# Relu-squared attention into a gated feed-forward block: the input loads issued in another order, with another order of the work behind them

## The chip, the cores and the metric

The kernel runs on one core of one Trainium2 chip. The metric is the time of one execution on the device, in microseconds (us). The profile is taken by the hardware profiler from one execution. The engines are named as in the profile: PE is TensorE (matmuls; PEld is its weight load), DVE is VectorE, ACT is ScalarE, POOL is GpSimd, and SP is SyncE. SPq and POOLq are the DMA issues of SP and POOL.

## The reference: what is computed

```python
# q, k, v: (8 batches, 12 heads, 448 tokens, 64)
scores = (1 / sqrt(64)) * matmul(q, k.transpose(0, 1, 3, 2))
attn = maximum(scores, 0.0) ** 2 / 448
x = matmul(attn, v)                     # heads joined: x is (3584 tokens, 768)
g = x @ w_gate                          # (768, 1536)
val = x @ w_val                         # (768, 1536)
out = (gelu(g) * val) @ w_out           # (1536, 768) -> (3584, 768)
```

The inputs and the output are float32; the kernel converts to bf16 as it loads.

## The kernel before, in words

**Tiles.** A batch has 12 heads, which are handled in three *thirds* of four heads; (b, m) is third m of batch b. Queries and keys of a third lie in one tile `qk16` (queries in the upper 64 partitions, keys in the lower), of which there are two buffers (`RING_H`). Values lie in `v16`, three buffers. Gate and value weights are cut into six pairs `wg0`/`wv0` to `wg5`/`wv5` of 256 columns each, the output weights into four tiles `wo0` to `wo3`. All matmuls use a quarter of the array (64 x 64), and four of them, in two rows and two columns, run side by side: `PE0` and `PE1` in the code are the two rows.

**Stages.** The head dimension has to be on the partitions for the scores, so queries and keys are transposed. For batches 0 and 1 TensorE does it (L641, copied by DVE at L645 into `qkT`). From batch 2 on (`EARLY = 2`) DVE regroups `qk16` into `qkr` (L477), and SP issues two DMA transposes per third from `qkr` into `qkT` (L482). Then come, for each third, seven units of scores (L693), a relu on ACT (L708, two banks, 128 x 896), the square on DVE (L717), the values (L763), and the scaled copy into `xT` (L779 or L790). Batches 0 and 1 do the gate and value matmuls plainly (`add_gate_value`, L995, with the gelu at L1002 and the product at L1007). From batch 2 on, half of those matmuls are done for two batches at once in seven products instead of eight, with sums of the weights (`ws`) and of the tokens (`ts`). The output product (`add_product`) takes 256 tokens at a time, also in seven products, with sums of the output weights (`wt`, L1047, which need `wo0` and `wo2`, or `wo1` and `wo3`).

**What sets the order.** The kernel holds a planner, `run_plan` (L96). Every step is an `Op` with an engine, a cost, dependencies and a lag (the time from its end until another engine can use its result). The planner simulates the engines, always takes the step that can start earliest, and emits instructions in the order in which it takes them. Each engine then runs its own instructions in that order. For batch 0 the order on TensorE is fixed by hand. Behind it, units of work are taken from a list, `LINE` (L12): `s` is the next score unit (or TensorE transposes) of its batch in turn, `o` a values unit, a digit a gate or value unit of that batch, `4A1` and the like a unit of the seven products for two batches, and `a1` to `n7` a unit of an output product. The planner takes the first unit among the next 60 that is ready, or, if none is, the one that will be ready first. Score units are always taken in their own order.

**Loads.** POOL issues all input loads, in program order, so a load that waits holds up all loads behind it. The planner counts a load's arrival from its bytes (L269):

```python
        if op in arrivals:
            dma = max(dma, op.end) + arrivals[op]
            op.lag = dma + 2.0 - op.end
```

The DMA transposes have a fixed lag of 5.0 (L494), and the score units that use them a margin of 1.5 for batch 2 and 3.0 later (L727). Some loads wait: a `qk16` tile for the readers of the tile two thirds before (TensorE's transposes, or DVE's regrouping), and later thirds also for relus, as a pace (L1385 to L1393): queries and keys from (2, 2) on for the first two relus of the third three places before, values from (2, 0) on for the fourth and sixth relu of the third two places before.

The order of the loads before, behind those of batch 0, is written out in L1242 to L1263: pair 0; (1, 0) all; pair 1; queries and keys of (1, 1); pair 2; values of (1, 1); queries and keys of (1, 2); pair 3; values of (1, 2); pairs 4 and 5; queries and keys of (2, 0) and (2, 1); values of (2, 0); the four output weights; queries and keys of (2, 2); values of (2, 1); and so on in turn.

Of the kernel before, what the change touches and what calls it, by code (L numbers as in the profile page):

```python
# [9 lines left out]


LINE = """  # L12
0 1 4A1 s 1 s 1 0 o 2 5 1 1 o d1 s 4C5 1 1 1 0 o 0 0 c5 s 2C1 s s o 3 s 0 s a1 s 0 1 2B4 o 5 2 g2
o s 3 0 2 b7 s 1 o 6B6 o s s s a5 a7 s 4B1 2 d4 s 0 0 0 0 o s 0 a2 4D1 2C7 s s s o 2E1 2A5 0 2C6 s
2A6 0 0 0 0 b5 0 s s 2 0 s 1 0 s s 1 a6 4E5 d7 2B1 2E2 1 0 o g6 1 f1 s 1 a4 c4 s s 4A2 1 b6 s s
2B6 s s 1 2D3 s o s s o d3 o c2 6B1 s s s 1 s s s 1 b2 s s b1 s s 1 s 3 1 s 2D6 1 c7 a3 s s 2E3 o
f5 o o 2E6 1 g7 1 2F1 b4 s 2B2 s 2A3 b3 2B3 c1 s o s 2F2 4 s s i5 3 c3 4F5 s s c6 s 2 2E7 2C3 2
2B5 2D1 s s 2F3 e6 2B7 s s s 2 3 2 s 2A1 2 6F4 g4 2A2 s 2A7 4E4 s 2A4 s o s s 4 e4 3 o d5 s s o
2D7 2D4 4A5 2C5 o 2D2 s o h2 2C2 2F6 s 2F7 2E5 s 5 f6 2D5 j2 2 4 4A4 4F6 s s 2C4 2F5 e2 s s 5 s
2F4 o 3 o 3 6B5 2E4 h4 2 s 4C1 m6 3 s 3 d6 s 6B2 s 4 3 s s n2 f3 f4 s o d2 o 3 4B4 4A7 6E1 s s e1  # L20
6B7 e7 o o 4B3 g1 s 7 4 6D6 s o f2 s e3 s 6E3 s 5 e5 s 4 6D3 7 m3 4D4 4E7 s m4 f7 s s 4 m5 4A6 s s
5 4 4B6 s 4B2 s s g5 i1 4C2 o o s s 4D2 4 4 s j5 s s j3 j1 s 6C6 g3 5 i7 6 s k5 6A2 o 4B7 s 4F2 5
4D5 4C6 4E2 4E1 s s 4B5 4A3 s s 4D3 s 4E6 6C7 4C3 s 6C3 o 4F3 6A1 4C7 s 4D6 s n1 l4 o s 6A7 s 4 k3
4C4 6 s o h1 4E3 i3 4D7 s h7 6A6 6E7 6 i4 s 4F1 j6 6 o 4 4F4 s n3 s 5 4F7 s i6 s s n5 s s 6D1 6 s
5 h6 s 5 o s 6A5 7 7 6D2 o s s 5 s h5 l7 6 s s 6C4 s n7 s 6E4 6A3 s o 6C1 6E6 i2 o 6E2 7 j7 7 s h3
l5 s s s 6B3 s l1 j4 s 7 6F2 6 s 6C2 k6 o k7 6 6F1 6D7 m7 6B4 7 6A4 6 6 m1 6F7 6 n6 6F6 k4 l2 6E5
m2 l6 k1 6 6D4 7 7 l3 7 7 6C5 6F3 6D5 6F5 n4 k2
"""


class Op:

    def __init__(self, engine, cost, emit, deps=(), lag=0.0, prio=0, other=None):
        self.engine, self.cost, self.emit, self.prio = engine, cost, emit, prio
        self.deps = [d for d in deps if d is not None]
        self.lag = lag
        self.other = other
        self.takes = None
        self.margin = 0.0
        self.after = None  # L40
        self.gates = []
        self.start = self.end = None
        self.place = 0
        self.open = False

# [50 lines left out]
def run_plan(queues, pools, units, banks, arrivals, together, fill):  # L96

    free = {e: 0.0 for e in (*queues, *pools)}
    at = {e: 0 for e in queues}
    dma = last = floor = busy = 0.0  # L100
# [108 lines left out]
    while left:  # L209
        best = None  # L210
        for e, ops in queues.items():
            if at[e] < len(ops):
                r = ready(ops[at[e]])
                if r is not None:
                    t = max(r, free[e], floor if e in together else 0.0)
                    key = (t, 0, free[e])
                    if best is None or key < best[0]:
                        best = (key, e, ops[at[e]])
        whole = at["PE0"] == len(queues["PE0"])
        if whole or at["PE0"] >= fixed:  # L220
            found = next_unit(not whole)
            if found is not None:
                key = (found[0], -1, free["PE0"])
                if best is None or key < best[0]:
                    best = (key, "PE0", found)
        for e, ops in able.items():
            mine = None
            for op in ops:
                r = ready(op)
                if r is not None:  # L230
                    t = max(r, free[e], floor if e in together else 0.0)
                    key = (t, op.prio, free[e], op.place)
                    if mine is None or key < mine[0]:
                        mine = (key, e, op)
            if mine and (best is None or mine[0][:3] < best[0][:3]):
                best = mine
        assert best is not None, "the plan is stuck"
        (t, *_), e, op = best
        if isinstance(op, tuple):
            _, u, k = op  # L240
            u.begun = True
            units.remove(u)
            for x in u.grabs:
                x.takes[0].ask(*x.takes[1:])
            if u.chain is not None:
                opened.add(u.chain)
                if u.name[-1] in "234":
                    opened.discard(u.chain)
            if k is not None:
                u.box["k"] = k  # L250
                banks[k] = u.closer()
            queues["PE0"][at["PE0"]:at["PE0"]] = u.los
            for n, hi in enumerate(u.his):
                hi.place, hi.open = u.los[0].place + n, True
                if not need[hi]:
                    able["PE1"].append(hi)
            op = u.los[0]
        if op.other is not None and e != op.engine:
            op.engine, op.cost, op.emit = op.other
        op.start = t  # L260
        op.end = t + op.cost
        free[e] = op.end
        if e in together:
            floor = t
            if t > busy:
                fill(busy, t)
            busy = max(busy, op.end)
        if op in arrivals:
            dma = max(dma, op.end) + arrivals[op]  # L269
            op.lag = dma + 2.0 - op.end  # L270
        if e in at:
            at[e] += 1
        else:
            for x in homes[op]:
                able[x].remove(op)
        if op.takes is not None:
            op.takes[0].take(*op.takes[1:])
        op.emit()
        for user in users.get(op, ()):
            need[user] -= 1  # L280
            if not need[user]:
                offer(user)
        last = max(last, op.end)
        left -= 1
# [4 lines left out]
def kernel(  # L289
# [21 lines left out]
    NM = NPAIR // 2  # L311
# [5 lines left out]
    FC = d_ff // 128  # L317
    WCH = 256
    NW = d_ff // WCH
# [3 lines left out]
    WOG = 3  # L323
# [2 lines left out]
    FB = 4  # L326
    FILL = 30.0
    EARLY = 2
    WO_AT = 2, 2, 2, 2

    NP = 3
    RING_V, RING_T, RING_H, RING_L, RING_A, RING_O, RING_E = 3, 3, 2, 2, 4, 4, 5
# [73 lines left out]
    def load_w12(i):  # L406
        cols = slice(i * WCH, (i + 1) * WCH)

        def emit(wt, src):
            return nc.gpsimd.dma_start(  # L410
                wt[:, :, :], src[:, cols].rearrange("(c p) f -> p c f", p=128))
        w12_op[i] = [load(4 * d_model * WCH, lambda wt=wt, src=src: emit(wt, src))
                     for wt, src in ((wg[i], moe_w_gate), (wv[i], moe_w_val))]
# [6 lines left out]
    def load_qk(b, i, h0, h1, deps=()):  # L420

        src = (q, k)[i]
        m, r0 = divmod(h0, 4)

        def tile_of():
            if (b, m) not in qk16:
                qk16[b, m] = hpool.tile([128, 4, SC * D], bf16, name="qk16", tag="qk16")
            return qk16[b, m][HALF[i], r0:r0 + h1 - h0, :]

        op = load(4 * (h1 - h0) * S * D, lambda: nc.gpsimd.dma_start(  # L430
            tile_of(), src[b, h0:h1].rearrange("h (p c) d -> p h (c d)", c=SC)),
            deps, rate=400e3 if b else 300e3)
        qk_loads.setdefault((b, m), []).append(op)
        for pr in range(h0 // 2, h1 // 2):
            head_op[b, pr, i] = op
# [14 lines left out]
            for pr in range(h0 // 2, h1 // 2):  # L450
                head_op[b, pr, 2 + i] = op

    def load_heads(b, h0, h1):
        load_qk(b, 0, h0, h1)
        load_qk(b, 1, h0, h1)
        load_v(b, h0, h1)

    qkT, tr_op = {}, {}

    def qkT_tile(b, m):  # L460
# [7 lines left out]
    def add_dma_transposes(b, m, deps=()):  # L468
# [12 lines left out]
        def emit_transpose(c0, c1):  # L481
# [3 lines left out]
            if b > EARLY and c0 or m and b == EARLY:  # L485
# [3 lines left out]
        n = len(regrouped)  # L489
# [2 lines left out]
        copy.margin = 3.0  # L492
        tr_op[b, m] = [Op("SP", 0.19 * 2 * (c1 - c0), lambda c0=c0, c1=c1: emit_transpose(c0, c1),
                          [copy], lag=5.0) for c0, c1 in ((0, VC), (VC, SC))]  # L494
        qk_used[b, m] = [copy]
        t_made[b, m] = [*tr_op[b, m]]
        if m or b > EARLY:
# [741 lines left out]
        if h0 > 2:  # L1239
            load_v(0, h0 - 4, h1 - 4)  # L1240
    load_v(0, 8, 12)
    load_w12(0)  # L1242
    load_heads(1, 0, 4)
    load_w12(1)
    load_qk(1, 0, 4, 8)
    load_qk(1, 1, 4, 8)
    load_w12(2)
    load_v(1, 4, 8)
    load_qk(1, 0, 8, 12)
    load_qk(1, 1, 8, 12)  # L1250
    load_w12(3)
    load_v(1, 8, 12)
    load_w12(4)
    load_w12(5)
    late = [(b, m) for b in range(2, B) for m in range(NM)]
    for n, (b, m) in enumerate(late):
        for i in range(FC // WOG):
            if WO_AT[i] == n:
                load_wo(i)
        for i in range(2):  # L1260
            load_qk(b, i, 4 * m, 4 * m + 4)
        for b_, m_ in late[n - 1:n] + (late[n:] if n == len(late) - 1 else []):
            load_v(b_, 4 * m_, 4 * m_ + 4)  # L1263
    add_weight_sums()
    for b, m in late:
        add_dma_transposes(b, m)
# [202 lines left out]
```

## Time and profile before

| | before |
|---|---|
| runs shown | 411.26, 412.3, 685.4 us; median 412.3 |
| the profiled execution | 411.88 us, of which the span of the profile is 410.1 |
| PE busy | 392.3 us (96%), 8477 instructions |
| DVE busy | 298.5 us (73%) |
| ACT busy | 244.8 us (60%) |
| POOL busy | 74.1 us (18%) |
| loads' queue (q0) | 24.39 MB in 37152 packets, 46.3% of 16 engines' span |
| stores' and transposes' queue (q1) | 19.08 MB in 37888 packets, 24.1% |
| chain that ended last | PE 91%, DMA 5% |
| mean granted TensorE clock | 0.985 |

The times are those of a whole execution; all places in time further on are counted from the start of the span. A row of the timeline gives the start, the duration, the engine, the line, the operation with what it writes and reads, the count, and in brackets how long the engine had been idle before and what released it. PE counts as busy while any matmul is in flight, so its share says nothing of how many of the four quarters are in use.

### The profile page before, as it was taken

To read this page: it belongs to the slowest core of one execution; us is meant where nothing else is said; L and a number is where in the kernel's file an instruction comes from. 1 tells how busy PE (TensorE), PEld (TensorE's weight loads), DVE (VectorE), ACT (ScalarE), POOL (GpSimd) and SP (SyncE) were. 2 spreads that over 40 slices of the span, in tenths; PEclk is the share of its full clock that TensorE was granted. 3 is DMA by queue.
4 is the path that set the end of the run, shared out by engine and by line. 5 is a ranking of instruction groups with operands and counts; after the bars stand their busy time and mean duration, and the time that the engine had idled before them with its cause. 6 is when DMAs were issued, how large, how long until landed. Compare 5 with 4: busy or idle time off the path is not lost.

```text
span 410.1 us, 18547 instructions
## 1 busy us (share of the span) xinstructions
PE 392.3 (96%) x8477; PEld 348.1 (85%) x8480; DVE 298.5 (73%) x513; ACT 244.8 (60%) x366; POOL 74.1 (18%) x120
## 2 busy tenths in 40 slices
PE   7999996499999999999999999999999999999994
PEld 3566785399989899989998999999999999989993
DVE  2976776198677978788877777688998766577562
ACT  5947783167677667786666676677776733242220
POOL 7756350111212211110111111111110000000000
PEclk9999999599999999999999999999999999999999
DMA  8999999987899799636498987765331411000245
GB/s 108 190 200 197 198 206 180 122 103 105 131 124 136 119 192 154 93 49 71 56 136 127 158 169 116 122 63 81 54 48 42 118 42 40 4 3 3 65 113 136
DMA packets 75278, 44.84 MB, mean 109 GB/s; under 512 B 36160, under 2 KB 71744, under 8 KB 75200
## 3 DMA queue, kind: packets, MB, share of 16 engines
q0 software_dynamic: 37152, 24.39, 46.3%
q1 hardware_dynamic: 37888, 19.08, 24.1%
q8 instruction: 66, 1.08, 1.1%
q10 hardware_dynamic: 160, 0.20, 0.1%
q14 instruction: 12, 0.10, 0.1%
HBM read 48.76 MB, written 11.01 MB: 146 GB/s over the span
## 4 chain that ended last, share of the span: by engine, by line
PE 91%; DMA 5%; ACT 1%; issue 1%; DVE 1%; SPq 0%; POOL 0%; POOLq 0%
PE ff L375 80%; PE sp L375 8%; DMA qkT<-qkr 4%; PE ff L562 1%; ACT attnT L708 1%; PE sp L641 1%; DMA qk<-in_k_dram 1%; PE ff L641 0%; DVE qkT L645 0%; DVE attnT L717 0%; PE ff L604 0%; ACT gel L1002 0%; DVE osb L1196 0%; SPq L482 0%; ACT qkT L612 0%
## 5 line engine op out<-in xcount | busy, mean ns | idle before, releaser
L375 PE MATMUL ff<-xT,wg 64*64 64x448 bf16 x1872 | 195.4, 351 | 0.0
L708 ACT ACTIVATE attnT<-sp 128x896 bf16<-128x896 f32 x168 | 151.6, 922 | 55.8 <-PE sp L375 53.4
L375 PE MATMUL ff<-xT,wv 64*64 64x448 bf16 x1440 | 156.3, 352 | 0.2 <-issue 0.2
L375 PEld LDWEIGHTS <-wv 64*64 64x64 bf16 x1872 | 115.3, 107 | 8.6 <-issue 0.9
L375 PEld LDWEIGHTS <-wg 64*64 64x64 bf16 x1872 | 113.7, 107 | 9.0 <-issue 0.2
L717 DVE TENSOR_TENSOR attnT<-attnT 128x1792 bf16<-128x1792 bf16 (+1 forms) x98 | 92.3, 953 | 12.6 <-ACT attnT L708 11.9
L375 PE MATMUL sp<-qkT 64*64 64x448 bf16 (+1 forms) x768 | 79.7, 330 | 10.1 <-DMA qkT<-qkr 9.0
L375 PEld LDWEIGHTS <-s 64*64 64x64 bf16 x1344 | 80.2, 107 | 4.4
L375 PE MATMUL ff<-attnT,v 64*64 64x448 bf16 (+1 forms) x768 | 83.7, 326 | 0.1
L375 PE MATMUL ff<-wo,s 64*64 64x384 bf16 x672 | 60.9, 323 | 0.0
L375 PE MATMUL ff<-wt,s 64*64 64x384 bf16 x672 | 60.8, 323 | 0.0
L1007 DVE TENSOR_TENSOR uT<-gel,ff 128x448 bf16<-128x448 bf16 x60 | 37.0, 617 | 31.2 <-PE ff L375 27.0
L375 PEld LDWEIGHTS <-uT 64*64 64x64 bf16 x912 | 55.2, 107 | 2.1
L375 PEld LDWEIGHTS <-qkT 64*64 64x64 bf16 x768 | 39.4, 106 | 16.5 <-issue 7.5
L445 POOL DMA_DIRECT2D v<-in_v_dram x48 | 29.5, 619 | 128.6 <-ACT attnT L708 98.2
L375 PE MATMUL ff<-ts,wv 64*64 64x448 bf16 x432 | 51.5, 349 | 0.0
L375 PE MATMUL ff<-ts,ws 64*64 64x448 bf16 x432 | 51.1, 349 | 0.0
L375 PEld LDWEIGHTS <-v 64*64 64x64 bf16 x768 | 46.9, 106 | 4.0 <-issue 1.0
L375 PE MATMUL ff<-wo,uT 64*64 64x384 bf16 x576 | 49.9, 323 | 0.0
L1002 ACT ACTIVATE gel<-ff 128x448 bf16<-128x448 f32 x60 | 32.5, 544 | 27.0 <-PE ff L375 26.9
L375 PEld LDWEIGHTS <-ws 64*64 64x64 bf16 x648 | 41.1, 106 | 2.3
L924 DVE TENSOR_TENSOR part<-ff,part 128x448 f32<-128x448 f32 x54 | 32.9, 620 | 11.8 <-PE ff L375 7.0
(60 smaller groups left out, 374.7 us busy)
## 6 DMA issues: line engine op xcount, KB each, us to landing
out_dram<-osb SPq DMA_DIRECT2D x54, 192.0 KB, 3.6
v<-in_v_dram POOLq DMA_DIRECT2D x48, 128.0 KB, 3.9
qk<-in_q_dram POOLq DMA_DIRECT2D x23, 224.0 KB, 4.9
qk<-in_k_dram POOLq DMA_DIRECT2D x23, 224.0 KB, 5.9
wg<-in_moe_w_gate_dram POOLq DMA_DIRECT2D x6, 384.0 KB, 10.3
wv<-in_moe_w_val_dram POOLq DMA_DIRECT2D x6, 384.0 KB, 11.2
wo<-in_moe_w_out_dram POOLq DMA_DIRECT2D x4, 576.0 KB, 13.5
qkT<-qkr SPq DMA_TRANSPOSE x36, 5.3
```

The source lines that it names most:

```text
L375: return nc.tensor.matmul(o, lhsT, rhs, start=start, stop=stop, skip_group_check=onto, tile_position=(P * row, P * col))
L445: return nc.gpsimd.dma_start(v16[b, m][HALF[i], :, :, :], v[b, h0:h1].rearrange("h (p c) d -> p h c d", c=SC)[:, :, c0:c0 + VC, :])
L562: nc.tensor.matmul(t[:, :], warm[:, 0:128], warm[:, :], start=True, stop=True)
L641: nc.tensor.transpose(t[HALF[j], c, :], src[:, 2 * r + j, c, :], ident[:, :], tile_position=(0, P * j))
L708: relu.ins = nc.scalar.activation(duo["a"][:, u % 2, :, :], box[0][:, :, 0:S], AF.Relu).ins
L717: nc.vector.tensor_tensor(a[:, part], a[:, part], a[:, part], op=ALU.mult)
L924: rd.ins = nc.vector.tensor_tensor(t[:, :], box[0][:, 0:S], t[:, :], op=ALU.add).ins
L1002: nc.scalar.activation(gel[b, fc][:, :], box[0][:, 0:S], AF.Gelu)
L1007: u_op[b, fc].ins = nc.vector.tensor_tensor(uT[b][:, fc, :], gel.pop((b, fc))[:, :], box[0][:, 0:S], op=ALU.mult).ins
```

## The change: what it does

1. The order of the loads behind batch 0 is read from a new string, `LOADS`. A `w` is the next pair of gate and value weights, `o` the next output weight in the order 0, 2, 1, 3, `q` the queries and keys of the next third from (1, 0) on, and `v` the values of the next third. Read out, it begins: pair 0; queries and keys of (1, 0) and (1, 1); values of (1, 0); pair 1; values of (1, 1); queries and keys of (1, 2) and (2, 0); pairs 2 and 3; values of (1, 2); queries and keys of (2, 1); pair 4; values of (2, 0); queries and keys of (2, 2); pair 5; values of (2, 1); output weight 0; queries and keys of (3, 0) and (3, 1); values of (2, 2); output weight 2; values of (3, 0); queries and keys of (3, 2); output weights 1 and 3; queries and keys of (4, 0) and (4, 1); and on. What each load waits for is as before.
2. The planner's lag of the DMA transposes is no longer fixed: if the loads counted so far keep the DMA queue busy beyond the end of the issue, the rest of that time is added (`queued`).
3. `LINE`, the order of the units, is replaced as a whole. It holds the same units.
4. `load_heads` and `WO_AT` go, as nothing uses them now. Each load gets a `token`, which nothing else uses.

```diff
 LINE = """
-0 1 4A1 s 1 s 1 0 o 2 5 1 1 o d1 s 4C5 1 1 1 0 o 0 0 c5 s 2C1 s s o 3 s 0 s a1 s 0 1 2B4 o 5 2 g2
...
+a6 4A4 4C4 s o 2 1 s g2 0 s 3 2C5 s 0 d3 o 0 2C1 4C1 s 1 4B6 s o s 0 0 0 s s 0 0 s s 0 s 2B2 s 2
...
+LOADS = """
+w q q v w v q q w w v q w v q w v o q q v o v q o o q q v q v q v v q v v q v q v q v q v q v q v
+q v v
 """
...
+        self.queued = False
...
         if op in arrivals:
             dma = max(dma, op.end) + arrivals[op]
             op.lag = dma + 2.0 - op.end
+        elif op.queued:
+            op.lag += max(0.0, dma - op.end)
...
+        for op in tr_op[b, m]:
+            op.queued = True
...
     late = [(b, m) for b in range(2, B) for m in range(NM)]
...
+    todo = {"w": [*range(NW)], "o": [0, 2, 1, 3], "q": [(1, m) for m in range(NM)] + late,
+            "v": [(1, m) for m in range(NM)] + late}
+    for x in LOADS.split():
+        n, at = len(POOL), todo[x].pop(0)
+        if x == "w":
+            load_w12(at)
+        elif x == "o":
+            load_wo(at)
+        elif x == "v":
+            load_v(at[0], 4 * at[1], 4 * at[1] + 4)
+        else:
+            for i in range(2):
+                load_qk(at[0], i, 4 * at[1], 4 * at[1] + 4)
+        for op in POOL[n:]:
+            op.token = x, at
+    assert not any(todo.values())
```

More of the change, by code (lines that the diff above doesn't have):

```diff
@@ L12 @@
 LINE = """
-0 1 4A1 s 1 s 1 0 o 2 5 1 1 o d1 s 4C5 1 1 1 0 o 0 0 c5 s 2C1 s s o 3 s 0 s a1 s 0 1 2B4 o 5 2 g2
[L14 to L27, printed above, removed]
+a6 4A4 4C4 s o 2 1 s g2 0 s 3 2C5 s 0 d3 o 0 2C1 4C1 s 1 4B6 s o s 0 0 0 s s 0 0 s s 0 s 2B2 s 2
+a2 b1 o 3 s 3 s 0 0 0 s 1 o s s 4B7 2B1 b4 0 0 0 1 0 0 s o s s s b5 a4 s b6 1 0 0 0 c2 f3 1 a7 o o
@@ new lines @@
+1 2B6 s s s 1 0 1 2C2 s s 2 2A3 s 1 1 2A5 2 1 f4 g4 s s s s 2E6 s 1 a3 c1 s 4 o 1 1 s f5 2B3 s 0 s
+d1 o s o 1 s 2F3 s s s s 1 2D1 1 1 c6 2D4 1 2F1 3 c3 2A1 s 6 c5 s 2F4 a1 2 s o 1 1 4C6 o o 2B4 a5
+1 2A2 1 s s b7 o 2D6 b3 s s e7 s d6 s s 2 s o c7 o b2 3 o 2 s 2A7 s 2B5 s 2B7 s o 2E4 s s s 2E2 s
+2 s 4A1 2D2 s s 4A2 2F5 s s 2C7 s 2A4 3 s c4 s e2 e4 o s 6B2 2F7 o 2 4F2 4B1 3 s 5 s 2D3 3 e1 s
+2F2 s 2E1 2A6 s 2F6 2E5 4B5 s 2C4 2D7 2C6 o 2D5 4B3 5 6 k4 s d5 d4 s l3 s f1 s o e5 4A5 2 d7 s 4
+4E4 2C3 2 g5 3 s h3 2E7 g6 s 6B4 o 2 s 4D1 o g7 s f2 3 s 2E3 f6 s 5 s 4 o d2 o e3 f7 4 s s s s 4
@@ new lines @@
+4D2 3 s e6 6A6 4 o s 6F1 4D7 s 4 4F6 3 6B1 g1 s s 4E1 s s l4 i1 6E6 o 4A3 4A6 4F5 4F4 o 6A4 o s g3
+s s h4 4D5 4C7 4A7 l7 i6 4E2 o n7 s o s 6C3 s 6B7 s s s 4 4B4 s s o 6 h2 6 6E5 s 4E5 s 5 4 4D3 4D4
+s s 7 o 7 6C7 s s s 4 s s s 4B2 4E7 s 6D5 5 4D6 6A3 h5 4E6 j6 m1 s 5 6 5 s s i3 4C5 5 l6 4 h7 s
+6F5 h1 4C2 6B3 l2 4F1 s 6F2 4C3 5 6B6 s n3 4 6D1 4F3 j1 4E3 k7 4F7 6C1 5 o s j3 6D6 o s m4 s 5 o
+6C5 o s i5 j5 i7 5 i4 6 s o i2 6E7 s j7 7 s 6B5 s 6 s m3 m5 6A7 s h6 s 6F7 6A1 j2 6D7 s s k3 s s o
+6 s s s m2 7 6A5 o n5 6F6 7 l5 j4 n4 6C2 s n6 s m7 m6 k1 k6 6A2 6 6F3 6 n2 7 6D2 6D4 k5 7 6E1 6C6
@@ L28 @@
+l1 6E2 6 7 6 6D3 7 6F4 7 7 k2 7 n1 6E3 6E4 6C4
+"""
+LOADS = """
+w q q v w v q q w w v q w v q w v o q q v o v q o o q q v q v q v v q v v q v q v q v q v q v q v
+q v v
 """
@@ L328 @@
     EARLY = 2
-    WO_AT = 2, 2, 2, 2
     NP = 3
@@ L451, in load_v @@
                 head_op[b, pr, 2 + i] = op
[L453 to L456, printed above, removed]
     qkT, tr_op = {}, {}
@@ L1241 @@
     load_v(0, 8, 12)
[L1242 to L1254, printed above, removed]
-    late = [(b, m) for b in range(2, B) for m in range(NM)]
[L1256 to L1263, printed above, removed]
+    late = [(b, m) for b in range(2, B) for m in range(NM)]
+    todo = {"w": [*range(NW)], "o": [0, 2, 1, 3], "q": [(1, m) for m in range(NM)] + late,
[14 more added lines that the diff above has]
+    assert not any(todo.values())
     add_weight_sums()
```

## The prediction

> **What bounds the kernel now.** I read the page's slices first, since a share of busy time hides where time is lost. The three rows are TensorE's busy share, its granted clock and the DMA share, in 40 slices of 10.25 us.
>
> ```profile
> PE   7999996499999999999999999999999999999994
> PEclk9999999599999999999999999999999999999999
> DMA  8999999987899799636498987765331411000245
> ```
>
> TensorE is the bound from about 50 us to 405 us: at 236 matmuls in 10 us (slice 90 to 100) there is nothing between them. The exceptions are the start, one hole in slices 7 and 8, and the last 5 us. The view of waits names the hole, and TensorE's timeline shows both ends of it:
>
> ```profile
> PE sp L375 <- DMA qkT<-qkr: 9.0, 1, 9.0
> ```
>
> ```profile
> 67.95 0.57 PE L375 MATMUL ff<-xT,wg 64*64 64x448 bf16 x6
> 77.53 0.96 PE L375 MATMUL sp<-qkT 64*64 64x448 bf16 x8 [9.01 <-DMA qkT<-qkr]
> 78.23 0.63 PE L375 MATMUL ff<-xT,wg 64*64 64x448 bf16 x2
> ...
> 82.13 0.38 PE L375 MATMUL ff<-xT,wg 64*64 64x448 bf16 x2
> ```
>
> Before and behind the wait stand gate matmuls of the same kind. TensorE had work; it runs its instructions in order, and the score matmul at the front needed batch 2's transposed queries and keys. Afterwards the same matmuls take 0.63 us and not 0.38 for some 3 us. The view of stretches gives that clock (after the times: the busy time and count of each engine, then the granted clock):
>
> ```profile
> 77.50:80.60 3.10, 3.07 (x36) 1.98 (x39) 0.00 (x0) 1.73 (x2) 1.03 (x2) 0.50 0.44 85
> ```
>
> The other engines' timeline shows why the transposes were late:
>
> ```profile
> 44.68 0.62 POOL L430 DMA_DIRECT2D qk<-in_k_dram  x1 [1.98 <-DMA v<-in_v_dram]
> ...
> 55.43 0.76 POOL L417 DMA_DIRECT2D wo<-in_moe_w_out_dram  x1 [0.36 <-DMA qk<-in_k_dram]
> 57.48 0.62 DVE L477 COPY qkr<-qk 128x1792 bf16<-128x1792 bf16 x1
> 58.21 8.66 SPq L482 DMA_TRANSPOSE qkT<-qkr  x2
> ```
>
> The keys, issued at 44.68, landed 10.5 us later at 55.2. The two transposes were issued at 58.21 and 59.58 and took 15.0 and 17.9 us, where the median of all 36 is 5.3. The last output weight, issued at 55.43, took 18.0 us, to 73.4; the transposes landed at 73.2 and 77.5. They came out with the loads around them. The old plan gave them the copy's end (58.1), 1.52 + 1.14 us on SP, a lag of 5 and a margin of 1.5, so 67.3; TensorE came to them at 68.5. The hole is a queue that the plan did not count.
>
> **What the change takes away.** Two things act on the hole. The transposes' lag now grows by what the DMA queue still holds, so TensorE's order leaves them more time. And batch 2's first third is loaded early. Adding the sizes in the order of issue (448 KB for queries and keys of a third, 256 for its values, 768 for a pair of weights, 576 for an output weight, 2112 before the first pair), that third ended at 9280 KB and now ends at 5952. Before, 5568 KB had landed at 35.7 us (third value weight: 24.66 + 11.0) and 6272 KB at 39.8 (keys: 29.66 + 10.1), so it should land at about 37, not 55. With the 3.0 us from landing to the transposes' issue, issue is near 40. Landing: the queue is as deep as the weights' own time to land, 10.3 to 12.9 us, and the second transpose came 4.1 us behind the last output weight; so 50 to 57 us, not 77.5. Batch 1's scores last until 62 us, so batch 2's would join on.
>
> Gain: 9.0 us of wait, and half of the 3.1 us at clock 0.50, 1.5 us. Together 10.5.
>
> **What the change delays.** The same sums give the weight pairs. The second pair moves from 4352 to 4800 KB, the third from 5568 to 6720, the fourth from 7040 to 7488, the fifth from 8064 to 8960, the sixth from 8832 to 10432. At 195 KB/us (slices of 198 to 200 GB/s) that is 2.3, 5.9, 2.3, 4.6 and 8.2 us later; before, their values landed at 29.4, 35.7, 43.6, 48.9 and 52.9. The transposes take DMA time too: of the 19.5 us from 58 to 77.5 their queue had 23%, 4.5 us for a third; over the run, where half the packets' time is output, under 2.4. So the fifth pair lands at 53.5 to 58 and the sixth at 61 to 70.
>
> A pair holds 96 gate and value matmuls of batch 0. Before, 190 had run by 40 us, and 192 need only two pairs: TensorE never waited for weights. Now the third lands at 41.6, so the cost is 0 (other work fills it) to 1.6 us; I take 0.7. By 53.4 us 365 had run, and 384 need the fifth pair: 0 to 3 us. By 60 us 474 had run, and 480 need the sixth, but batch 1's gates can start once its last values are scaled (65.9 us before, near 62 after), on pairs already there: 0 to 2 us. I take 0.7 for both, close to nothing, since batch 2's scores are ready in the same stretch.
>
> **What else is moved on POOL, SP and TensorE.** Batch 1's second third comes before the second pair: 3776 KB, landing near 26.4 instead of 31.7. Its transposes on TensorE stand ahead of batch 1's scores (before: transposes at 32.27, first relu at 33.39), so that chain starts 3 to 4 us earlier. TensorE does only 206 matmuls between 30 and 40 us against 224 and 228 later, about 1 us that could be filled; I take -0.6. The queries of (2, 0) reuse the buffer that those transposes read, and the third and fourth pairs now stand behind them on POOL. If the transposes stayed at 32.3 to 33.9 us, the queue would run dry (5504 KB is through at 35.2, a start-up of a few us): 0 to 2 us, contained in the range. The wait for (1, 2)'s transposes (42.4 before) falls while 7744 KB are good until 47: nothing. (2, 2) waits for batch 1's 16th relu (56 before, 52 after) with the sixth pair behind it, while 9216 KB are good until 55: nothing. SP's transposes move earlier, ahead of any store (the first store is at 107.7): nothing. The assertion and the tokens issue nothing.
>
> Sum against the profiled execution's 411.9 us: -10.5 + 0.7 + 0.7 - 0.6 = -9.7, so 402.2. The profiled execution lies 0.4 below the median of 412.3, so I keep 402.2.
>
> **Rivals.** *The wait moves and shrinks* (0.22). TensorE's order now expects the transposes when the counted queue is empty plus 6.5 us. If only 7744 KB are counted (43 to 45 us), that is about 50, and they land at 50 to 57: a wait of up to 7 us, or 3 to 6 with what fits between, so 405 to 409. What speaks for it is that the plan counts no DMA time for the transposes themselves. A mechanism that would give it: loads and transposes alternate packet by packet, whatever is ahead. From 58 to 77.5 us there were 1856 packets of the transposes and 2602 of loads; alternating, the transposes are through after 3712 of 4458, 16 us from issue, and the order of the loads would not shorten that as long as the loads keep coming: 40 + 16 = 56, against 50 a wait of 6, 408. The Trainium skill (DMA: Bandwidth & Descriptors, "Queues, rings and completion order") says that each DMA engine goes round its queues packet by packet, which is this rule. The landings at 73.2 and 77.5 fit both; the trace does not part them.
>
> *The output weights come too late* (0.10): the case for slower. Before, all four stood ahead of (2, 2)'s queries. Now the second and last wait behind (3, 2)'s keys, which wait for batch 2's 16th relu. That was 29.8 us after its first (78.16 to 107.92). With a first relu at 57, issue is at 87 to 88, landing 9.6 us later, four sums of 0.75 us: products from 100 (86.7 before). Without products TensorE has attention for batches 0 to 2 (7.9 us each: 144 matmuls of four per 0.189 us and 48 at half), their early transposes (4 us), and 1152 gates (54.4 us): 82 us, on top of 18 lost by 40 us; it is dry at 100. Batch 3's scores add up to 8. So it costs nothing if batch 2's scores keep their pace. If they are stretched as filler to 50 us or more, products start past 120, TensorE waits 12 to 20 us, and the time is 414 to 422. The turning point is products after 118 us.
>
> *It does nothing* (0.06): the scores still stand in front of a landing that comes 10 us late, only elsewhere: 409 to 413.
>
> My forecast, the hole gone, has 0.62: 399 to 405.
>
> **How the numbers follow.** A difference of 2% is about what a measurement of this kernel tells from no change: 8.2 us, so faster means under 404.1. Nine tenths of my forecast's 399 to 405 lie there: 0.56. Slower is over 420.5, the lower chance of the second rival and accidents that I don't see: 0.08. The rest, 0.36, is the same. The range starts at 398.5 (no cost for the weights, all of the early gain, 0.4 us and a clock that never falls) and reaches to 413, which takes in the first and third rival and leaves out the second.
>
> **What would show it.** Right: no wait of TensorE for the transposes over 2 us, granted clock 0.9 or more in every slice after the first, batch 2's first scores between 50 and 62 us, its first transposes issued near 40. The first rival shows as a wait for the transposes of 3 us or more; the second as products after 100 us and a hole there; late weights as a wait of gate matmuls on wg or wv between 40 and 66 us. I am wrong if a hole of 8 us or more is left anywhere before 400 us.

## The result, and the profile after

| | before | after |
|---|---|---|
| runs, us | 411.26, 411.43, 412.3, 685.4 | 415.89, 415.99, 416.14, 417.43 |
| median, us | 411.87 | 416.06 |
| profiled execution, us (its span) | 411.88 (410.1) | 416.14 (414.3) |
| mean granted TensorE clock | 0.985 | 0.988 |

The changed kernel takes 1.0114 times as long, with a 95% interval of 1.0083 to 1.0146: slower by about 4.7 us. The forecast was 402.2, the range 398.5 to 413. Some kernels further on scattered from run to run: the ratios of p_noq (four of ten) and after_w5sp (four of seven) go by their undisturbed runs alone, and the profiles of after_w5, after_sp, after_w5sp, p_noq and before_early are of longer runs (414.8, 415.2, 417.7, 414.4 and 409.7 us).

The page's slices of the kernel after (10.36 us each; TensorE's busy share, its clock, the DMA share) show no hole any more:

```profile
PE   7999987998999998999999999999999999999994
PEclk9999998998999999999999999999999999999998
DMA  7999999599959789844197899747420511000335
```

In place of a 6 and a 4 in TensorE's row stand an 8 and a 7, an 8, and another 8. The view of waits gives the small stops behind them (total us, times, longest):

```profile
PE ff L382 <- issue: 4.2, 4, 1.9
PE sp L382 <- DMA qkT<-qkr: 2.1, 1, 2.1
PE ff L382 <- DMA wv<-in_moe_w_val_dram: 1.9, 1, 1.9
...
PE ff L382 <- DMA wg<-in_moe_w_gate_dram: 0.9, 1, 0.9
...
PE ff L382 <- DMA wo<-in_moe_w_out_dram: 0.5, 1, 0.5
```

The 9.0 us wait for (2, 0) is gone: its transposes were issued at 42.54 and 43.90 and had landed by 57.4. The 2.1 us are another third's, (2, 2). Add the five lines and it is 9.6 us, a little more than the one wait before. TensorE's timeline has the places (in brackets the idle time before, and what ended it):

```profile
54.27 0.35 PE L382 MATMUL ff<-attnT,v 64*64 64x448 bf16 x1 [1.47 <-issue]
...
64.46 0.57 PE L382 MATMUL ff<-xT,wg 64*64 64x448 bf16 x6 [0.95 <-DMA wg<-in_moe_w_gate_dram]
...
68.52 0.38 PE L382 MATMUL ff<-xT,wv 64*64 64x448 bf16 x2 [1.92 <-DMA wv<-in_moe_w_val_dram]
...
96.83 0.59 PE L382 MATMUL sp<-qkT 64*64 64x448 bf16 x4 [2.07 <-DMA qkT<-qkr]
...
164.60 0.35 PE L382 MATMUL ff<-ts,wv 64*64 64x448 bf16 x1 [1.87 <-issue]
...
171.35 0.35 PE L382 MATMUL ff<-ts,ws 64*64 64x448 bf16 x1 [0.57 <-issue]
```

Each of the two groups that waited for data is followed by the low clock. The stretches behind them (busy time and count of PE, PEld, DVE, ACT, POOL, then clock, DMA share, GB/s):

```profile
70.00:72.00 2.00, 2.00 (x28) 1.90 (x22) 0.00 (x0) 1.60 (x3) 0.00 (x0) 0.50 1.18 202
98.00:100.00 2.00, 2.00 (x28) 1.30 (x24) 1.49 (x4) 0.45 (x1) 0.61 (x1) 0.50 0.51 100
```

28 matmuls in 2 us, where an undisturbed stretch has some 48, and TensorE still reads as fully busy. So waits alone understate the loss. I therefore counted the matmuls in each 10 us, gave a group of four side by side 0.187 us per 448 columns (the pace of the full stretches), and called the rest lost. A full stretch comes out at -0.2, so the count runs some 2% high in work:

| stretch, us | lost before | lost after | what it is after |
|---|---|---|---|
| 0 to 50 | 18.3 | 18.1 | the start, as before |
| 50 to 60 | -0.3 | 1.8 | stop without a releaser, 1.47 |
| 60 to 70 | 1.6 | 3.8 | sixth pair of weights, 0.95 + 1.92 |
| 70 to 80 | 8.7 | 1.3 | before: the hole; after: low clock |
| 80 to 90 | 0.3 | -0.3 | |
| 90 to 100 | -0.2 | 3.6 | transposes of (2, 2), 2.07, and low clock |
| 100 to 160 | 0.1 | 0.8 | first output weight, 0.46 |
| 160 to 180 | -0.4 | 2.5 | two stops without a releaser, 1.87 + 0.57 |
| sum to 180 | 28.0 | 31.7 | |

By 100 us the hole's time has been given back, as far as such a count can tell: 28.4 us lost before, 28.3 after. From there to 180 us the changed kernel loses 3.7 us more, and that is the difference of the spans (4.2) within half a microsecond.

Why the weights were late is in POOL's timeline:

```profile
47.52 0.63 POOL L452 DMA_DIRECT2D v<-in_v_dram  x1 [4.67 <-ACT attnT L712]
...
53.48 0.61 POOL L437 DMA_DIRECT2D qk<-in_q_dram  x1 [3.57 <-ACT attnT L712]
55.27 0.80 POOL L437 DMA_DIRECT2D qk<-in_k_dram  x1 [1.18 <-issue]
56.07 0.83 POOL L417 DMA_DIRECT2D wg<-in_moe_w_gate_dram  x1
56.89 0.83 POOL L417 DMA_DIRECT2D wv<-in_moe_w_val_dram  x1
```

First the values of (2, 0) waited for relus (their pace; 4.67 us, and 1.15 more for the second half), then the queries of (2, 2), and the sixth pair stood behind them all. With the keys, for which no releaser is seen, POOL was idle for 10.6 us ahead of the pair. The pair's two loads then took 8.3 and 11.6 us, to 64.4 and 68.5: the two moments at which TensorE went on. Why (2, 2)'s transposes were late is in SP's timeline. Its first one was issued at 76.35; then come:

```profile
83.91 1.94 SPq L484 DMA_TRANSPOSE qkT<-qkr  x1
...
90.12 1.21 SPq L484 DMA_TRANSPOSE qkT<-qkr  x1
```

The row at 83.91 is the first transpose of (3, 0), which waited for its regrouping on DVE (the copy at 83.23 to 83.85), although (2, 2)'s first had landed at 80.94. The row at 90.12 is the second of (2, 2), whose data had been regrouped at 63.69. The kernel lets a third's second transpose start only when the transpose issued before it has landed, and (3, 0)'s first, which the plan had put between (2, 2)'s two, landed at 90.10. So the second of (2, 2) started 9.2 us after the first had landed, 3.0 of them for a copy and 6.2 for a landing that it did not need; it landed 6.6 us later, at 96.7.

### The profile page after: what moved, and what is told of

Its sections match the earlier page's. It is cut to its first block, busy times and chain, and to the rows that moved or that the text cites. A ratio compares the mean times of both kernels' runs of the same rounds, so it can differ in the third digit from the quotient of the medians.

```text
span 414.3 us, 18542 instructions
## 1 busy us (share of the span) xinstructions
PE 395.9 (96%) x8480; PEld 337.4 (81%) x8480; DVE 299.8 (72%) x515; ACT 244.8 (59%) x364; POOL 74.5 (18%) x120
## 3 DMA queue, kind: packets, MB, share of 16 engines
q8 instruction: 66, 1.08, 1.1%
## 4 chain that ended last, share of the span: by engine, by line
PE 80%; DMA 13%; issue 3%; POOL 2%; ACT 1%; DVE 0%; POOLq 0%
PE ff L382 71%; PE sp L382 7%; DMA v<-in_v_dram 3%; DMA qkT<-qkr 3%; DMA wv<-in_moe_w_val_dram 3%; DMA wo<-in_moe_w_out_dram 2%; POOL qk L437 1%; DMA qk<-in_k_dram 1%; PE sp L645 1%; ACT attnT L712 1%; PE ff L566 1%; PE ff L645 1%; POOL v L452 0%; DVE osb L1200 0%; POOL ident masks.py:199 0%
## 5 line engine op out<-in xcount | busy, mean ns | idle before, releaser
L382 PE MATMUL ff<-xT,wg 64*64 64x448 bf16 x1872 | 189.7, 353 | 1.0 <-DMA wg<-in_moe_w_gate_dram 0.9
L382 PEld LDWEIGHTS <-wv 64*64 64x64 bf16 x1872 | 107.4, 107 | 17.7 <-issue 3.2
L382 PEld LDWEIGHTS <-wg 64*64 64x64 bf16 x1872 | 107.1, 108 | 15.3 <-issue 2.4
L382 PE MATMUL sp<-qkT 64*64 64x448 bf16 (+1 forms) x768 | 74.8, 331 | 2.6 <-DMA qkT<-qkr 2.1
L382 PEld LDWEIGHTS <-s 64*64 64x64 bf16 x1344 | 74.3, 107 | 3.3
L382 PE MATMUL ff<-wo,s 64*64 64x384 bf16 x672 | 62.5, 323 | 0.0
L382 PEld LDWEIGHTS <-uT 64*64 64x64 bf16 x912 | 52.9, 107 | 3.0 <-issue 1.1
L382 PE MATMUL ff<-wt,s 64*64 64x384 bf16 x672 | 52.6, 323 | 0.0
L382 PEld LDWEIGHTS <-qkT 64*64 64x64 bf16 x768 | 35.7, 107 | 9.7 <-issue 5.6
L382 PEld LDWEIGHTS <-ws 64*64 64x64 bf16 x648 | 39.0, 106 | 5.4 <-issue 0.9
L1006 ACT ACTIVATE gel<-ff 128x448 bf16<-128x448 f32 x60 | 32.6, 543 | 18.2 <-PE ff L382 17.9
```

Source lines behind the costliest of these rows:

```text
L382: return nc.tensor.matmul(o, lhsT, rhs, start=start, stop=stop, skip_group_check=onto, tile_position=(P * row, P * col))
L1006: nc.scalar.activation(gel[b, fc][:, :], box[0][:, 0:S], AF.Gelu)
```

## The experiments

Unless said otherwise, a kernel's plan is made unchanged, and behind its first 32 us the list of planned steps is kept, a few steps in it are moved by hand, and then it is emitted. So only the order on the engine named differs:

```diff
-        op.emit()
+        if script or t > 32.0:
+            script.append((e, op, op.emit))
+        else:
+            op.emit()
...
+    move(...)            # the moved steps, and the step that they are put ahead of
+    for _, _, emit in script:
+        emit()
```

**The two orders.** The sixth pair moved ahead of the values of (2, 0) on POOL (after_w5); the second transpose of (2, 2) moved ahead of the first of (3, 0) on SP (after_sp); both (after_w5sp).

```diff
+    move([("w", 5)], ("v", (2, 0)))
+    move([("t", (2, 2), 1)], ("t", (3, 0), 0))
```

> The changed kernel with every engine's planned order kept, except that POOL issues the sixth pair of gate and value weights right behind the fifth, ahead of the loads that wait for batch 1's relus. Theory (the sixth pair is late because it stands behind a waiting load): the waits for wg and wv between 62 and 68.5 us and the lowered clock from 70 to 73 go, 3.8 + 1.3 us of lost TensorE time, so 5 us faster, near 411. Rival (TensorE only comes sooner to the scores of (2, 1), whose transposes are issued one at a time and land at 68 and 76 us): a wait for qkT takes its place and less than 1 us is gained.

> The changed kernel with every engine's planned order kept, except that SP issues the second transpose of (2, 2) ahead of the first of (3, 0). Theory (the wait at 94.8 to 96.8 us is this transpose standing behind one that waits for its regrouping copy at 83.2): it is issued near 81 us, the wait of 2.1 us and the lowered clock from 97 to 100 go, 3.5 us of lost TensorE time, near 412.5. Rival (the transposes of (3, 0) become the late ones): the wait moves to about 100 us, gain under 1 us.

> Both edits together. Theory: the gains add, 8 to 9 us, near 407.5; what is left against 402 are the stops of TensorE at 52, 163 and 171 us that no data explain. Rival: the gains don't add, because the second wait grows when TensorE arrives earlier; 410 or more.

Against the kernel before they measured 1.0011 (0.9983 to 1.0039), 1.0004 (0.9976 to 1.0033) and 0.9955 (0.9925 to 0.9986). Taken from 1.0114 that is 4.2, 4.5 and 6.5 us gained, each to within some 1.7 us by the two intervals. In after_w5 no gate or value matmul waits for a weight, but the wait for (2, 2) has grown (timeline of after_w5):

```profile
94.95 0.59 PE L397 MATMUL sp<-qkT 64*64 64x448 bf16 x4 [4.01 <-DMA qkT<-qkr]
```

and in after_sp it is the other way round, no wait for transposes and a longer one for the sixth pair:

```profile
68.02 0.79 PE L397 MATMUL ff<-xT,wg 64*64 64x448 bf16 x6 [2.86 <-DMA wg<-in_moe_w_gate_dram]
```

Each order costs about 4 us, where the prediction took 0.7 for the fifth and sixth pair together and nothing for SP's order. That is 1.5 and 2.2 times the idle time that the waits view shows for them (2.9 and 2.1 us). Both edits gain 6.5 and not 8.7; the difference of 2.2 lies within the noise of the four ratios (some 2.4). In the profiled run of after_w5sp other stops take the place of the two waits, as its waits view shows:

```profile
PE ff L398 <- issue: 6.5, 4, 2.9
PE ff L398 <- DVE attnT L738: 2.5, 2, 2.2
```

How much of that is in its runs of 409 to 412 us is not shown.

**The stops without a releaser.** All of them in the kernel after lie at the same place of TensorE's instruction stream: matmuls 859, 3031, 3159 and 4566 are its instructions 1730, 6082, 6338 and 9155, which are 194, 194, 194 and 195 above a multiple of 256. The instruction queue's row of the page has 66 packets and 1.08 MB, so 16 KB each. TensorE's 16960 matmuls and weight loads make 257 for a packet, so a packet is taken here as a block of 256 instructions. after_shift splits the dummy matmuls of the warm-up and of the first gaps into four each, which puts 96 more matmuls ahead and pushes the block ends onto other matmuls (the edit for the warm-up):

```diff
-                nc.tensor.matmul(t[HALF[j], :], warm[:, HALF[j]], warm[:, :],
+            for c in range(4):
+                for j in range(2):
+                    nc.tensor.matmul(t[HALF[j], c * 128:(c + 1) * 128], warm[:, HALF[j]], warm[:, 0:128],
```

> The changed kernel with TensorE's dummy matmuls at the start and in its first gaps cut into four each (128 columns instead of 512, the same columns in all); every other instruction keeps its place. TensorE's instruction stream behind them moves on by 192 instructions. Theory (the stops that the profile calls issue lie where TensorE needs the next block of 256 instructions): they stay at the same place in a block, so they lie at other matmuls than at 859, 3031 and 3159 of the changed kernel, 96 earlier or 32 later; total within 1% of the changed kernel. Rival (a wait for data): they stay at the same matmuls.

It measured 1.0157 (1.0113 to 1.0201). Its stops of 0.3 us and more after 50 us are at instructions 1986, 6338, 8642, 9410 and 10690 of the longer stream, each again 194 above a multiple of 256, and none is at a matmul at which the kernel after stops. The place in the block decides, not the work.

before_load asks whether loads are what makes the blocks late. It is the kernel before with 72 loads more behind its last one, into buffers that nothing reads any more:

```diff
+    for _ in range(36):
+        spare = hpool.tile([128, 4, SC * D], bf16, name="qk16", tag="qk16")
+        for i, src in enumerate((q, k)):
+            nc.gpsimd.dma_start(spare[HALF[i], :, :], src[0, 0:4].rearrange("h (p c) d -> p h (c d)", c=SC))
```

> The kernel before, with 72 more loads behind its last one (queries and keys of (0, 0), 224 KB each, into the two qk16 buffers, which nothing reads any more). They are issued from about 303 us on, where the kernel before moves little (DMA digits 1 to 4) and TensorE stops for nothing, and each waits for the one two places before it in the same buffer, so that up to four are in flight. No matmul waits for them and no instruction of TensorE, ACT, DVE or SP is changed. Theory: TensorE's stops without a releaser are blocks of 256 of its instructions that come late because loads fill the DMA engines; then such stops appear between 305 and 390 us, at the same place in each block as in the kernel after (193 to 195 of 256), several of 0.3 to 2 us, 2 to 5 us with the clock behind them: 414 to 418. Rival: the blocks come late for another reason (the place in the code, a branch, the start of the program), and loads do nothing to them: no stop over 0.3 us there, 411 to 413. A third way to the longer time would be that the stores of the output are slowed and TensorE waits for a bank that ACT or DVE has not emptied: then the wait names ACT or DVE.

The time of 436.17 us (1.0547, 1.0508 to 1.0586) says nothing of the question: the loads were meant to end before the kernel does, but they went on to 434 us, and the execution waits for them. TensorE's last matmul is 4.4 us later than in the kernel before (408.8 against 404.3), 1.7 of it lost ahead of the added loads (it is that much behind at 250 us). Behind the first of the added loads (304.7 us) the timeline has three stops where the kernel before has none:

```profile
328.12 0.28 PE L375 MATMUL ff<-attnT,v 64*64 64x224 bf16 x1 [0.28 <-issue]
...
398.59 1.71 PE L375 MATMUL ff<-wt,s 64*64 64x384 bf16 x34 [1.04 <-issue]
...
401.67 0.35 PE L375 MATMUL ff<-wt,uT 64*64 64x384 bf16 x2 [0.52 <-ACT osb L1196]
```

The first two are at block ends; the third names ACT and lies behind the second. That is 1.3 us of stops at block ends, and TensorE falls some 1.9 us further behind over the two: at the low end of the theory's 2 to 5, and more than the rival's none. One more stop, 0.31 us at 241.82, is at a block end too, ahead of the added loads; its packet lagged 3.7 us, against 2.8 in the kernel before. The records of the packets decide between theory and rival. The earliest packets of blocks begin when TensorE is 63 instructions short of the end of a block; taking that as the moment of the request, a packet's lag is how much later it begins:

| kernel | packet (from 0) | begins, us | lag, us | from its end to TensorE's use, us | stop, us |
|---|---|---|---|---|---|
| before | 7 | 62.1 | 3.5 | 1.4 | none |
| before | 17 packets, 303 to 398 us | | 0.3 mean, 1.1 at most | 3.0 to 5.2 | none |
| before_load | 16 packets, 303 to 398 us | | 1.7 mean, 4.2 at most | 1.5 to 4.8 | see below |
| before_load | 51 | 325.7 | 3.7 | 1.6 | 0.28 |
| before_load | 63 | 396.2 | 4.2 | 1.5 | 1.04 |
| after | 5 | 51.5 | 5.0 | 1.6 | 1.47 |
| after | 22 | 162.0 | 5.7 | 1.6 | 1.87 |
| after | 23 | 168.2 | 3.6 | 1.4 | 0.57 |

The loads raise the mean lag from 0.3 to 1.7 us in the same stretch of the same program, so they are the cause there. A stop ends 1.4 to 1.6 us after the packet has landed, and every stop in the table follows a lag of 3.6 us or more. That fits the pace: a block lasts 5.2 to 6.2 us when nothing stops TensorE, and a lag of 3.6, the packet's 1.0 and another 1.4 make 6.0. The kernel before was at that limit: its packet 7 left nothing to spare, and packet 8 (68.4 us, lag 3.9) came while TensorE stood in the hole. But the hole did not hide much. p_q_only (below) has the loads of the kernel before and no hole: its packets 7, 8 and 9 lagged 3.6, 3.9 and 4.1 us, and there is one stop, 0.53 us at 77.45. So most of the changed kernel's 4.2 us had not been behind the hole: packets 5 and 22 lag 5.0 and 5.7 us in it, against 3.1 and 2.5 in the kernel before, which had no hole at either place.

**What the transposes wait for.** In before_wo, the kernel before with the output weights moved behind the keys of (2, 2) on POOL (and two sums of them behind, on DVE), the transposes of (2, 0) are issued before any output weight.

```diff
+    move([("o", 0), ("o", 2), ("o", 1), ("o", 3)], ("v", (2, 1)))
+    move([("wt", 3, 0), ("wt", 2, 0)], ("wt", 4, 0))
```

> The kernel before with every engine's planned order kept, except that POOL issues the four output weights (in the order 0, 2, 1, 3) behind the queries and keys of (2, 2), and DVE makes the first two sums of output weights right before the third. Theory (the transposes of (2, 0) wait for the bytes that were issued ahead of them): at 58.2 us some 9984 KB instead of 12288 stand ahead, so they land near 63 to 65, TensorE comes to them at 68.5, the 9.0 us wait and the lowered clock go, 401 to 402. Rival (loads and transposes alternate packet by packet, so a transpose takes 16 us wherever loads keep coming): it still lands near 74 to 76, gain 1 to 3 us.

It measured 0.9938 (0.9917 to 0.9959). The first transpose, issued at 59.55, landed after 5.3 us. The second was issued at 60.92. Then POOL issued the output weights:

```profile
61.19 3.00 POOL L435 DMA_DIRECT2D wo<-in_moe_w_out_dram  x4
```

and the second transpose took 13.5 us, to 74.4, where TensorE stood for it:

```profile
74.45 0.96 PE L391 MATMUL sp<-qkT 64*64 64x448 bf16 x8 [4.62 <-DMA qkT<-qkr]
```

So loads that were issued behind a transpose slow it too: in before_hold (next), where no output weight is issued until it has landed, the same transpose took 7.6 us. It shares the engines with whatever is in flight, and does not wait in a line. The Trainium skill (DMA: Bandwidth & Descriptors, "Queues, rings and completion order") has each DMA engine go round its queues packet by packet; 7.6 against 13.5 us agrees with it.

before_hold issues the output weights behind the values of (2, 1) and keeps them back until the second transpose has landed.

```diff
+            tc.add_manual_dep(ins.ins, landed[HOLD].ins.name, SYNC, reason="pace")
```

> The kernel before with every engine's planned order kept, except that POOL issues the four output weights behind the values of (2, 1) and, by an added wait, only when the second transpose of (2, 0) has landed; DVE makes the first two sums of output weights right before the third. Theory (transposes and loads take turns on the DMA engines, so a transpose is slow while loads of any age are in flight, and quick, 5.3 us, when there are few): it lands near 66 us, TensorE comes to it at 68.5, the 9 us wait goes, 401 to 403. Rival (the time of the transposes only moves: those of (2, 1) now meet the output weights and come late): a wait of 4 to 8 us near 83 us takes its place, 406 to 410.

It measured 1.0081 (1.0046 to 1.0117). No matmul waits for a transpose, and the wait stands at the output product instead, with a second behind it (timeline):

```profile
84.15 0.53 PE L396 MATMUL ff<-wo,uT 64*64 64x384 bf16 x2 [5.74 <-DMA wo<-in_moe_w_out_dram]
...
89.08 0.58 PE L396 MATMUL ff<-xT,wg 64*64 64x448 bf16 x2 [3.77 <-DVE uT L1041]
```

before_early keeps the old list of units and the old lag. It loads the queries and keys of (2, 0) ahead of the sixth pair, regroups them earlier, and puts the output weights where before_wo has them.

```diff
+    move([("q", (2, 0))], ("w", 5))
+    move([("c", (2, 0))], ("ws", 4, 2))
+    move([("o", 0), ("o", 1), ("o", 2), ("o", 3)], ("v", (2, 1)))
+    move([("wt", 3, 0), ("wt", 2, 0)], ("wt", 4, 0))
```

> The kernel before with every engine's planned order kept, except for POOL and DVE: the queries and keys of (2, 0) are loaded ahead of the sixth pair of weights, DVE regroups them three instructions earlier, the output weights (0, 1, 2, 3) are loaded behind the queries and keys of (2, 2), and the first two sums of output weights are made right before the third. Theory (a transpose is slow only while loads are in flight, and the queue runs low at 58 us, where the next load waits for a relu): issued near 54.5 us, the transposes land by 62, ahead of the output weights' issue at 61 and of TensorE's 68.5; the 9.0 us wait and the lowered clock go, less 1 to 3 us for output weights that land near 78 with the first product at 77: 402 to 405. Rival (the DMA engines have no time left before 80 us, so every earlier transfer makes another late): a wait of 5 us or more for output weights or weights in its place, 407 to 412.

It measured 0.9881 (0.9852 to 0.9911), 407.41 us: the fastest here, faster than both kernels. No matmul waits for a transpose or a weight from 50 us on. What is left in the timeline:

```profile
69.92 0.35 PE L393 MATMUL ff<-attnT,v 64*64 64x448 bf16 x1 [3.59 <-issue]
...
84.79 0.32 PE L393 MATMUL ff<-wo,uT 64*64 64x384 bf16 x1 [1.05 <-issue]
```

Both are block ends: the packet for the first began 7.0 us after its request, at 67.2, with the four output weights in flight (issued from 58.47, 12.6 to 21.4 us to land); the packet for the second began 3.0 us late and itself took 2.7. Four small moves do what the whole change was after, and the late block takes back 3.6 us of it.

**The parts of the change, each planned anew.** p_q_only has the lag that counts the queue, with the old loads and list; p_loads_only the new loads alone; p_line_only the new list alone; p_noq loads and list without the lag; noq_w5 is p_noq with the sixth pair moved as in after_w5.

```diff
 p_noq, against the kernel after
-            op.queued = True
+            op.queued = False
 p_q_only, against the kernel before
+        elif op.queued:
+            op.lag += max(0.0, dma - op.end)
```

> The old order of loads and the old list of units; of the change only the longer lag of the DMA transposes in the plan, which is made anew. Theory (the plan's old lag alone made the hole): the scores of batch 2 move back in TensorE's order and the 9 us wait shrinks to under 3 us, 402 to 406. Rival (the list was searched for the old lag, so the new plan runs out of other work or is in a worse order later): within 1% of the kernel before.

> The changed kernel, planned anew without the longer lag of the transposes (fixed 5 us as before); new order of loads and new list of units. Theory (the longer lag is what made the plan put the second transpose of (2, 2) behind the first of (3, 0), and otherwise helped): that inversion goes, but TensorE comes to batch 2's transposes too early by 5 to 10 us, 416 to 424. Rival (with the early loads the lag does not matter): within 1% of the changed kernel.

> The old list of units and the fixed lag with the new order of loads, planned anew. Theory (the new order of loads makes the sixth pair late whatever the list): TensorE waits for wg or wv between 60 and 70 us, no wait for the transposes of (2, 0) over 2 us, 410 to 418. Rival (list and loads belong together; either alone is worse): 420 or more, with waits past 100 us.

> The new list of units with the old order of loads and the fixed lag, planned anew. Theory (the hole comes from the loads and the lag, not the list): a wait for the transposes of (2, 0) near 68 to 78 us of 6 us or more stays, 410 to 416. Rival (the new list alone moves batch 2's scores behind other work): a wait under 3 us, 404 to 408.

> The changed kernel planned anew with the fixed lag of the transposes, that order kept, and the sixth pair of weights issued right behind the fifth. Theory (late sixth pair and inverted transposes are the two largest losses of the change): neither wait is there, 404 to 407, 2% below the changed kernel. Rival (the DMA engines are full until 85 us and a transfer that is early makes another late): waits of 4 us or more between 60 and 100 us for other data, 409 or more.

| | ratio to before | 95% | where TensorE stands, us |
|---|---|---|---|
| p_q_only | 1.0228 | 1.0202 to 1.0253 | relus, 4.1 in five waits from 100 to 159 |
| p_loads_only | 1.0267 | 1.0218 to 1.0316 | wg 3.42, a square 2.24, v 1.42, wo 1.40 |
| p_line_only | 1.0305 | 1.0283 to 1.0328 | transposes of (2, 0) 7.97, relus 3.5 |
| p_noq | 0.9968 | 0.9936 to 1.0000 | wg 2.17, wv 1.9, block ends 2.9 |
| noq_w5 | 1.0127 | 1.0035 to 1.0219 | a square 4.63, wo 1.93, block ends 2.3 |

In p_q_only the hole is gone as well, and in p_loads_only no matmul waits for a transpose either: the lag or the loads alone remove it. In p_q_only the plan now puts batch 2's scores later, and attention becomes the late one (timeline):

```profile
111.77 0.38 PE L381 MATMUL sp<-qkT 64*64 64x448 bf16 x4 [1.10 <-ACT attnT L711]
```

In p_line_only the hole stays:

```profile
77.82 0.96 PE L381 MATMUL sp<-qkT 64*64 64x448 bf16 x8 [7.97 <-DMA qkT<-qkr]
```

So each part alone makes it worse than the whole does: a list of units goes with one order of loads. p_noq lacks the inversion on SP, so the counted lag brought it. Its interval reaches up to no change, but its ten runs lie between 408.0 and 423.0, so what the lag is worth within the change stays open.

noq_w5 was to add after_w5's 4 us to p_noq, and gained nothing: its four runs (414.5 to 422.0) lie within the spread of p_noq's ten. DVE's timeline shows what took the place of the waits:

```profile
68.77 0.63 DVE L494 COPY qkr<-qk 128x1792 bf16<-128x1792 bf16 x1 [5.42 <-issue]
69.31 0.62 DVE L737 TENSOR_TENSOR attnT<-attnT 128x896 bf16<-128x896 bf16 x1
```

The copy regroups a third whose keys were issued at 55.22 and took 13.5 us, to 68.7 (in p_noq 7.4 us, to 63.6). The square behind it, for which TensorE stood 4.63 us, needed nothing but its turn: ACT's last relu ahead of it had ended at 66.1. The sixth pair put earlier made these keys later, and an in-order engine passed that on to unrelated work.

## Why the prediction was wrong

**Right: the hole goes (-10.5).** (2, 0)'s transposes were issued at 42.54 (predicted near 40) and landed by 57.4 (50 to 57), and no matmul waited for them. Batch 2's first scores are at 61.84 (77.53 before), just inside the 50 to 62 expected; its first relu, taken as 57, came at 65.33 (78.16 before). The rival's rule of alternating packets, 16 us from issue, was right about the landing (14.9 us) and before_wo bears it out, but the wait that it was to bring did not come, as TensorE got to those scores at 61.84, and not at the 50 us that the rival took.

**Right: the third pair, and the output weights.** Up to 50 us the loss is the same, 18.1 against 18.3, within the 0 to 1.6 us given. The first output products come at 108.16, later than the 100 worked out but below the turning point of 118, and cost 0.46 us of waiting.

**Wrong: "(2, 2) waits for batch 1's 16th relu ... with the sixth pair behind it, while 9216 KB are good until 55: nothing."** The pair was issued at 56.07 and landed at 64.4 and 68.5, inside the 61 to 70 that the prediction itself had worked out. The cover was what failed. Batch 1's gates were to start "near 62"; its relus did begin 3 us earlier (30.42 against 33.39) but ended at 61.76, as before (62.16), and the last scaled copy of its values, without which none of its gates can be finished, came at 69.7 (65.9 before). So the -0.6 fell as well, and when TensorE ran out of weights, at 63.5 and 66.6, batch 1's gates could not fill in. after_w5 prices the step at 4.2 us against the 0 to 2 given: the wait and the low clock after it.

**Wrong: "SP's transposes move earlier, ahead of any store: nothing."** The stores were the wrong thing to look at. SP's queue holds transposes that wait for DVE, and the new lag let the plan put (3, 0)'s first between the two of (2, 2): in p_noq, without that lag, (2, 2)'s two follow each other. after_sp prices it at 4.5 us.

**Missing: TensorE's own instructions.** Nothing in the sum counted them, since the profile before shows no such stop. In the kernel after they are 4.2 us of idle time. The prediction asked which data would be late next; it did not ask what loads in a new order would do to the packets of TensorE's instructions. No run here takes these stops out of the changed kernel, so what they cost in all is not shown.

**The range.** Its upper end, 413, took in one small wait at a time. All three came at once, and their idle time was as large as the hole. By the runs, both orders (6.5 us), the stops (4.2) and the 0.6 that was not gained, less the 1.4 that the sum had set aside for weights, make some 10 of the 13.9 us between 402.2 and 416.1; it is a rough sum, as the stops differ from kernel to kernel, and the rest stays open. "Granted clock 0.9 or more in every slice" failed in three slices, the last of the span among them, and "a wait of gate matmuls on wg or wv between 40 and 66 us" is what happened, at 64.46 and, a little past it, at 68.52.

## What to carry to other kernels

While the DMA engines are full, putting one load forward puts another back: before counting a removed hole as gained, list every load that falls behind a paced one, every queue that an earlier step can now block, and the packets of instructions that the loads hold up. Where an in-order engine has a step ahead that can wait, what stands behind it pays even if its own data are there. A hand edit of a few steps in an otherwise unchanged plan measured more here (0.9881) than a new plan with three parts, each of which made it slower when planned alone.

## What the runs showed of the hardware

TensorE's instructions come as 16 KB packets on a DMA queue of their own, and loads hold them up: 72 more loads raised their mean lag from 0.3 to 1.7 us. A packet takes about 1 us (2.7 at most in the rows above), TensorE went on 1.4 to 1.6 us after it had landed at the stops above, and with the engines full it began up to 7.0 us after the request, while TensorE uses up a block in 5.2 to 6.2 us. The Trainium skill (Runtime: NRT & Kernel Launch, "Instruction fetch mechanics") gives the blocks of 256 instructions, with which the 66 packets agree, and calls the crossing mostly hidden; here it cost up to 3.59 us.

A DMA transpose of about half a third took 5.3 us in the median of 36 in the kernel before. With loads in flight it took 10.5 to 17.9 us (kernel after from 42.54 to 57.54, kernel before at 58.21 and 59.58), and 13.5 also where the loads came behind it (before_wo).
